# A long convolution beside a feed-forward on one core: copies of x and loads of w2 moved to later places in a planned order

## The chip, the cores and the metric

The kernel runs on one core of a Trainium2 chip. The metric is the device time of one execution in microseconds (us). Times are medians of several runs; the profile comes from one more execution, whose own time is given beside its span (from its first to its last instruction). The engines are TensorE (PE; PEld is its loading of weights), VectorE (DVE), ScalarE (ACT), GpSimd (POOL) and SyncE (SP). SP computes nothing here: it issues nearly all DMAs, in one queue, in order. POOL issues the DMAs that add into memory.

## The reference

The input x has 2048 rows of 1024 columns, in float32. Its rows are normalized (mean 0, variance 1), and two results are added to x:

```python
xn = _layernorm(x, axis=-1)
k_shift = 4-tap causal depthwise convolution of k        # per channel
kv = k_shift * v
y = causal depthwise convolution of kv with ssm_k        # 2048 taps, per channel, by FFT
a = xn * (y + kv * ssm_D)
b = silu(xn @ w1) @ w2                                   # 1024 -> 3584 -> 1024
return x + a + b
```

## The kernel before

**The feed-forward** is the work of TensorE. Every float32 operand is split into a high and a low float16 part, and three products stand for one. The first GEMM goes through w1 in 14 pairs of column tiles (`i`, 256 columns each) and the rows in two halves (`sp`, 1024 rows each). Most pairs run as a *unit*: seven products of sums of blocks (a Strassen scheme) in place of eight, 84 matmuls of 128x512 in all (`units`). The sums of x and w1, their split and the taking out of the products are work of VectorE and ScalarE. The order is two plain pairs for the first half, then 12 units for the first half, then 14 units for the second. `flag["unit", i]` is set where unit `i` of the second half begins. Hidden blocks go out to DRAM (`hs`, `hsf`) and come back as blocks `wo`.

The second GEMM begins when all units are done (`feed_forward`, from `flag["gemm1"]` on). It goes through the two column halves `h` of the result; in each, for 16 row tiles `t`, five blocks of 4 hidden tiles are summed in PSUM, and `result(h, t, ...)` scales the sum, and adds it into the result in DRAM (a POOL DMA with `accum_op`, helper `G`, L331 to L333). The last four pairs of hidden tiles follow as a second Strassen part (`units2`).

**The scale of w2.** Each pair of row tiles of w2 is scaled by a power of two that comes from the norms of w1 and w2. For the norms alone, `squares_w2` loads all of w2 once, in 28 pieces of 512 KB, into a buffer `wraw` or (for the first seven pairs) `yt`, and ScalarE squares and sums each piece. When all are done, `norms_w2` makes the scales (`tau`, `invc`), and then w2 is loaded once more (`load_w2`), scaled and split for the second GEMM.

**The convolution** goes in 8 groups of 128 channels. For one group k, v and the long filter are loaded; VectorE and ScalarE apply the taps and multiply with v (`gate`); the signal is split (`cm`) and turned by four transposing DMAs on SP's queue (helper `X`, L326 to L329, into `hl`); TensorE makes the first stage of a Fourier transform (`stage1`, L1490 to L1492); VectorE does the rest of it, the product and most of the inverse (`forward`, `product`, `inverse`, in the buffers `spec` and `tmp`); a norm sets the scale of the result (`result_scales`); the parts are split (`zh`, `zl`); TensorE does the last stage (`stage1_inv`, L1682 to L1684); VectorE multiplies with the scale and the normalized x (`gated`, into `yt`, `xg` being the rows of x), and POOL adds the 8 pieces of a group into the result. In the profile nearly all operations of VectorE have the lines of two helpers (L336, L339) and those of ScalarE one (L347), so they are told apart by buffer names.

**The result starts as a copy of x.** `copies` issues 16 DMAs from x to the result, each of 256 rows and one column half (512 KB): eight for the first column half, then eight for the second. `flag["copied", half]` lets the convolution's adds of that column half go ahead: groups 0 to 3 lie in the first half, 4 to 7 in the second.

**What sets the order.** All engines' instructions are written out by a planner (`Order`, L106 to L194). Each strand of work is a generator that yields an operation with a planned cost, or a condition to wait for. The planner always takes the strand whose next operation can begin first in its model, less a bias, and emits it. So a condition, or a planned cost, changes the place of everything after it, on all engines, though the engines themselves run only by their queues and semaphores. In the model a DMA occupies one common pipe for its `nbytes` at 330 GB/s. A strand's conditions are conditions of the planner alone: they set no semaphore.

Of the kernel before, what the change touches and what calls it, by code (L numbers as in the profile page):

```python
# [25 lines left out]
NT = S // P  # L26
# [79 lines left out]
class Order:  # L106
# [27 lines left out]
    def add(self, gen, bias, floor=0.0):  # L134
        s = Stream(gen, bias, floor)
        self.streams.append(s)
        self.advance(s)
# [151 lines left out]
def h3_ffn_kernel(ctx, tc, x, kp, vs, fs, shift, dskip, w1, w2, cfwd, cinv, out):  # L289
    nc = tc.nc  # L290
# [3 lines left out]
    flag = defaultdict(Token)  # L294
# [12 lines left out]
    def size(a):  # L307
        n = 1
        for s in a.shape[1:]:
            n *= s  # L310
        return n
# [10 lines left out]
    def L(o, i, m=0.3):  # L322
        n = size(o) * o.shape[0] * mybir.dt.size(o.dtype)
        return Op("SP", 0.4, 0.1, lambda: nc.sync.dma_start(o, i), [i], [o], m, n)

    def X(o, i, m=0.3):  # L326

        n = size(o) * o.shape[0] * mybir.dt.size(o.dtype)
        return Op("SP", 0.6, 0.1, lambda: nc.sync.dma_start(o, i, transpose=True), [i], [o], m, 1.5 * n)  # L329

    def G(o, i, m=0.3):  # L331
        n = size(i) * i.shape[0] * mybir.dt.size(i.dtype)
        return Op("POOL", 1.1, 3.0, lambda: nc.gpsimd.dma_start(o, i, accum_op=ADD), [i], [o], m, n)  # L333
# [8 lines left out]
    def a_act(o, i, func, scale=1.0, bias=None, total=None):  # L342
        def f():
            kw = {} if bias is None else {"bias": bias}
            if total is not None:
                kw["accum_out"] = total
            nc.scalar.activation(o, i, func, scale=scale, **kw)  # L347
        ins = [i] + [s for s in (scale, bias) if s is not None and not isinstance(s, float)]
        p = A(f, o, ins)
        p.table = func if func in (AF.Sqrt, AF.Silu) else None  # L350
        p.busy += 0.07 * (len(ins) - 1) - 0.06 * (i.space == bass.MemoryType.PSUM)
        if total is not None:
            p.busy += 0.19
            p.writes.append(total)
        return p
# [566 lines left out]
    def plain_unit(i, b, xf, ready, m=1, free=False):  # L922

        ph = []
        for j in range(2):
            yield ff.ready
            ph.append(ff.tile([P, 4, P]))
        for n, j in [(n, j) for n in range(m) for j in range(2)]:
            q = slice(n * 4 // m, (n + 1) * 4 // m)
            for a in range(2):  # L930
                for r in ready[a][n * len(ready[a]) // m:(n + 1) * len(ready[a]) // m]:
                    yield r
                yield flag["w", "plain", i, a, j]
                w, tok = wops["plain", i, a, j]
                yield from steps(ph[j][0][:, q, :], w, xf[a][:, q], a == 0, a == 1)
                if free and n == m - 1:
                    tok.set()
            if n == m - 1:
                if j == 0:
                    hf, both = yield from places_of(i, b)  # L940
                add(silu(i, hf[:, j], *ph[j], both), EB)
# [11 lines left out]
    def units():  # L953

        todo = [(i, 0) for i in range(2, NP)] + [(i, 1) for i in range(NP)]
        yield ff.ready
        one = ff.tile([P, 4, P])
        yield from product("P1", *todo[0], one[0], True)
        for n, (i, sp) in enumerate(todo):
            if sp == 1:  # L960
                flag["unit", i].set()
                flag["room", 1].set()
            if i in PAIRS:
                add(quad(i, sp), 0.1)
            made, seen = defaultdict(Token), defaultdict(Token)
            yield ff.ready
            c = ff.tile([P, 4, P])
            add(evacuate(i, 2 * sp, one, c, made, seen), EB)
            yield from product("P7", i, sp, c[0], True)
            yield seen["P1"]  # L970
            two = seen["bank"][0]
            yield from product("P6", i, sp, two)
            made["P6"].set()
            yield from product("P2", i, sp, one[0])
            made["P2"].set()
            yield seen["P6"]
            yield from product("P5", i, sp, two)
            made["P5"].set()
            if n + 1 < len(todo):
                yield ff.ready  # L980
                one = ff.tile([P, 4, P])
                yield from product("P1", *todo[n + 1], one[0], True)
            yield seen["P5"]
            yield from product("P3", i, sp, two)
            made["P3"].set()
            yield seen["P7"]
            yield from product("P4", i, sp, c[0])
            made["P4"].set()
# [13 lines left out]
    def feed_forward():  # L1002
        first = [xo[0]["A11"], xo[0]["A12"]]
        r = [flag["rows", t] for t in range(4)]
        yield from plain_unit(0, 0, first, (r, r), 2)
        yield from plain_unit(1, 0, first, ((), ()))
        yield flag["x", 0, "A22"]
        lower = [second["A21"], xo[0]["A22"]]
        r = [(flag["x", 0, "A21"],), (flag["x", 0, "A22"],)]
        yield from plain_unit(0, 1, lower, r, free=True)  # L1010
        yield from plain_unit(1, 1, lower, r, free=True)
        second["tok"].set()
        flag["room", 0].set()
        yield from units()
        flag["gemm1"].set()
        for h in range(2):
            for ts in TOGETHER[h]:
                pos = {}
                for c in range(NC):
                    for t in ts:  # L1020
                        if c == 0:
                            yield ff.ready
                            pos[t] = ff.tile([P, W])
                        yield flag["h", h, t, c]
                        hx, htok = flag["h", h, t, c].what
                        yield flag["w2", h, c]
                        wc, wtok = w2c[h, c]
                        yield from steps2(pos[t][0], hx, wc, c == 0, c == NC - 1)
                        htok.set()
                        if t == NT - 1:  # L1030
                            wtok.set()
                        if c == NC - 1:
                            add(result(h, t, *pos[t]), EB)
        flag["last part"].set()
        yield from units2()

# [4 lines left out]
    def steps2(po, hx, wc, first, last, more=False):  # L1041
        for n in range(4):
            def mm(n=n):
                kw = dict(skip_group_check=more)
                nc.tensor.matmul(po, hx[:, n, 0, :], wc[:, n, 0, :], start=first and n == 0, stop=False, **kw)  # L1045
                nc.tensor.matmul(po, hx[:, n, 0, :], wc[:, n, 1, :], start=False, stop=False, **kw)  # L1046
                nc.tensor.matmul(po, hx[:, n, 1, :], wc[:, n, 0, :], start=False, stop=last and n == 3, **kw)  # L1047
            yield T(mm, po, [hx[:, n], wc[:, n]], 3 * 0.2185)
# [112 lines left out]
    def result(h, t, po, tok):  # L1161
        yield vs_r.ready
        o, otok = vs_r.tile([P, W])
        yield a_act(o, po, AF.Copy, invc[:, 0:1])
        tok.set()
        yield G(orr[t // T2, t % T2, :, h * W:(h + 1) * W], o)
        otok.set()
# [14 lines left out]
            flag["h2", u, n].set()  # L1182

    def copies():
        for a in range(NT):
            yield flag["unit", a // 2]
            n = NT // 2
            q = slice(a % n * 2 * P, (a % n + 1) * 2 * P), slice(a // n * W, (a // n + 1) * W)
            o = out[q]
            yield Op("SP", 0.4, 0.1, lambda: nc.sync.dma_start(o, x[q]), [], [], 0.3, P * D * 4)  # L1190
            flag["copied", a // n].set()

    def squares_w2():

        yield lambda: "wraw" in ctxs
        for i in range(NP):
            for h in range(2):
                yield lambda: any(r.pairs() for r in ctxs["squares"][i])
                raw, tok = next(r for r in ctxs["squares"][i] if r.pairs()).pair([P, 2, W])
                yield L(raw, w2r[:, 2 * i:2 * i + 2, h * W:(h + 1) * W])  # L1200
                add(square_w2(raw, tok, ss2[:, i, h:h + 1]), 0.01)
# [3 lines left out]
    def square_w2(raw, tok, o):  # L1205
        yield a_act(raw, raw, AF.Square, total=o)
        tok.set()
        flag["w2 squares"].set()
# [556 lines left out]
    add(factors_w1(), 0.04)  # L1765
    add(spill_w1(), 0.0)
    add(feed_forward(), 0.0)
    add(load_x(), 0.06)
    add(load_h(), 0.05)
# [45 lines left out]
```

## Time and profile before

| | |
|---|---|
| median of 3 runs | 1280.41 us (1280.33 to 1281.85) |
| the profiled execution | 1279.35 us, span 1277.5 us |
| granted TensorE clock, mean | 0.989 |
| busy: PE, DVE, ACT, POOL | 1236.3, 1150.4, 729.8, 132.8 us |
| moved by DMA | 292.94 MB, mean 229 GB/s |

The first GEMM's matmuls run from 15 to 592 us, the first convolution group's first stage begins at 302.5 us, the last group's at about 1147 us. Busy times are of engines that work side by side; idle time of an engine costs only where another one waits for it. A row with `[1.52 <-ACT cm L347]` at its end says that the engine was idle for 1.52 us before it and which instruction ended that.

### The profile page before, as it was taken

How to read it: one execution, taken by the hardware profiler on the slowest of the kernel's cores; microseconds unless marked ns; L12 is line 12 of the kernel's file. 1: busy time of each engine (PE TensorE's matmuls, PEld its weight loads, DVE VectorE, ACT ScalarE, POOL GpSimd, SP SyncE). 2: the span in 40 equal slices, each digit the busy share in tenths (PEclk: the TensorE clock that was granted, in tenths of full speed). 3: DMA queues.
4: the chain of work that ended last, by engine and by line, in shares of the span. 5: the costliest groups of instructions: out<-in, count | busy, mean ns of one | idle time of the engine just before them, and what ended most of it. 6: DMA issues, size and time to landing. Idle time of an engine off the chain costs nothing.

```text
span 1277.5 us, 17092 instructions
## 1 busy us (share of the span) xinstructions
PE 1236.3 (97%) x6018; PEld 596.9 (47%) x6018; DVE 1150.4 (90%) x1533; ACT 729.8 (57%) x1169; POOL 132.8 (10%) x141
## 2 busy tenths in 40 slices
PE   7899999999899999999999999999999999999994
PEld 6544444444344454444444444444454454445442
DVE  8999997898599969999799979989979988998996
ACT  6867987777775577666654452364263246535232
POOL 0000000000000030000210120030030021112213
PEclk8999999999899999999999999999999999999998
DMA  9447899889999899888996696598677678977865
GB/s 329 157 158 230 269 323 313 287 261 344 340 367 303 283 268 291 242 237 278 321 293 159 152 224 148 105 279 265 138 162 205 148 156 257 232 168 143 156 107 75
DMA packets 253894, 292.94 MB, mean 229 GB/s; under 512 B 48752, under 2 KB 167536, under 8 KB 251632
## 3 DMA queue, kind: packets, MB, share of 16 engines
q1 hardware_dynamic: 227072, 266.93, 67.0%
q0 software_dynamic: 26736, 24.92, 15.1%
q8 instruction: 47, 0.77, 0.2%
q14 instruction: 39, 0.32, 0.1%
HBM read 193.22 MB, written 98.57 MB: 228 GB/s over the span
## 4 chain that ended last, share of the span: by engine, by line
PE 59%; DVE 21%; DMA 7%; issue 7%; ACT 2%; POOL 2%; SPq 0%; POOLq 0%; DVEq 0%; ACTq 0%
PE ff L918 12%; PE ff L919 12%; PE ff L917 12%; DVE spec L336 8%; PE ff L1045 6%; PE ff L1047 6%; PE ff L1046 6%; DVE tmp L336 3%; DMA out<-yt 2%; DVE spec L339 2%; POOL out L333 2%; DVE x L339 1%; PE ps L1490 1%; PE ps L1492 1%; PE ps L1491 1%
## 5 line engine op out<-in xcount | busy, mean ns | idle before, releaser
L1045 PE MATMUL ff<-x,wo 128*128 128x512 f16 x864 | 327.4, 379 | 2.9 <-ACT hf L347 1.7
L1046 PE MATMUL ff<-x,wo 128*128 128x512 f16 x864 | 327.4, 379 | 0.2 <-DVE x L339 0.2
L1047 PE MATMUL ff<-x,wo 128*128 128x512 f16 x864 | 327.4, 379 | 0.0
L917 PE MATMUL ff<-x,wo 128*128 128x512 f16 (+1 forms) x808 | 305.2, 378 | 2.0 <-ACT hf L347 1.8
L918 PE MATMUL ff<-x,wo 128*128 128x512 f16 (+1 forms) x808 | 305.1, 378 | 2.0 <-DVE x L339 2.0
L919 PE MATMUL ff<-x,wo 128*128 128x512 f16 (+1 forms) x808 | 305.1, 378 | 0.3 <-DVE wo L339 0.3
L336 DVE TENSOR_TENSOR spec<-spec 128x512 f32<-128x512 f32 (+2 forms) x256 | 261.4, 1053 | 2.2
L1046 PEld LDWEIGHTS <-wo 128*128 128x128 f16 x864 | 84.5, 98 | 103.0 <-issue 3.7
L1047 PEld LDWEIGHTS <-wo 128*128 128x128 f16 x864 | 84.5, 98 | 102.4 <-issue 0.5
L1045 PEld LDWEIGHTS <-wo 128*128 128x128 f16 x864 | 85.4, 99 | 99.7
L919 PEld LDWEIGHTS <-wo 128*128 128x128 f16 x808 | 79.7, 99 | 96.2 <-issue 3.5
L917 PEld LDWEIGHTS <-wo 128*128 128x128 f16 x808 | 81.3, 101 | 88.4 <-issue 0.8
L918 PEld LDWEIGHTS <-wo 128*128 128x128 f16 x808 | 79.8, 99 | 91.1 <-issue 3.3
L347 ACT ACTIVATE hf<-ff,invc 128x512 f32<-128x512 f32 x64 | 43.6, 682 | 117.5 <-PE ff L1047 80.4
L333 POOL DMA_DIRECT2D out<-yt x62 | 69.5, 1312 | 344.3 <-DVE yt L339 200.8
L333 POOL DMA_DIRECT2D out<-hf x63 | 56.1, 890 | 459.3 <-ACT hf L347 393.7
L336 DVE TENSOR_TENSOR tmp<-spec 128x2048 f32<-128x2048 f32 (+1 forms) x48 | 92.4, 1934 | 1.0
L347 ACT ACTIVATE spec<-spec 128x1024 bf16<-128x1024 f32 x32 | 33.8, 1055 | 81.1 <-DVE spec L336 81.0
L339 DVE SCALAR_TENSOR_TENSOR ht<-hf,wsc,ht 128x1024 f16<-128x1024 f32 (+1 forms) x56 | 67.4, 1204 | 11.0 <-ACT ht L347 10.8
L339 DVE SCALAR_TENSOR_TENSOR acc<-kin,taps,acc 128x1024 f32<-128x1024 f32 x48 | 61.5, 1281 | 11.9 <-ACT acc L347 11.4
L347 ACT ACTIVATE ht<-hf,wsc 128x1024 f16<-128x1024 f32 (+1 forms) x56 | 60.8, 1085 | 6.0 <-DMA hsfA<-ht 2.6
L347 ACT ACTIVATE spec<-ps 128x512 f32<-128x512 f32 x93 | 52.7, 588 | 18.7 <-PE ps L1492 17.9
(177 smaller groups left out, 1744.0 us busy)
## 6 DMA issues: line engine op xcount, KB each, us to landing
wo<-hs SPq DMA_DIRECT2D x160, 256.0 KB, 3.5
hs<-ht SPq DMA_DIRECT2D x80, 256.0 KB, 5.2
out<-hf POOLq DMA_DIRECT2D x63, 256.0 KB, 4.3
wraw<-in_w SPq DMA_DIRECT2D x30, 512.0 KB, 5.9
raw<-in_w SPq DMA_DIRECT2D x28, 512.0 KB, 5.8
kin<-in_kp SPq DMA_DIRECT2D x16, 704.0 KB, 6.0
xt<-in_x SPq DMA_DIRECT2D x16, 512.0 KB, 7.4
kf<-in_fs SPq DMA_DIRECT2D x8, 1024.0 KB, 7.0
```

The lines of the kernel that those rows point to most:

```text
L333: return Op("POOL", 1.1, 3.0, lambda: nc.gpsimd.dma_start(o, i, accum_op=ADD), [i], [o], m, n)
L336: return V(lambda: nc.vector.tensor_tensor(o, a, b, op=op), o, [a, b], **k)
L339: return V(lambda: nc.vector.scalar_tensor_tensor(o, a, s, b, op0=op0, op1=op1), o, [a, b] + ([] if isinstance(s, float) else [s]), **k)
L347: nc.scalar.activation(o, i, func, scale=scale, **kw)
L917: nc.tensor.matmul(o, w[:, 0, k], xf[:, :, k, 0], start=first and k == 0, stop=False, **kw)
L918: nc.tensor.matmul(o, w[:, 0, k], xf[:, :, k, 1], start=False, stop=False, **kw)
L919: nc.tensor.matmul(o, w[:, 1, k], xf[:, :, k, 0], start=False, stop=last and k == KH - 1, **kw)
L1045: nc.tensor.matmul(po, hx[:, n, 0, :], wc[:, n, 0, :], start=first and n == 0, stop=False, **kw)
L1046: nc.tensor.matmul(po, hx[:, n, 0, :], wc[:, n, 1, :], start=False, stop=False, **kw)
L1047: nc.tensor.matmul(po, hx[:, n, 1, :], wc[:, n, 0, :], start=False, stop=last and n == 3, **kw)
L1490: nc.tensor.matmul(o, cf[:, 0], hi[i], start=i == 0, stop=False, **kw)
L1491: nc.tensor.matmul(o, cf[:, 0], lo[i], start=False, stop=False, **kw)
```

## The change

Three edits, of which the last two are new conditions for the planner and the first a planned cost:

- The transposing DMA is planned with its own bytes instead of 1.5 times as many.
- The copies into the second column half no longer follow the units; copy number `a - 8` of that half waits until the plan has added `result(0, t)` for row tile `t = a - 8` of the first column half.
- The loads of w2 for its norms wait for `flag["unit", 2]`, the begin of the third unit of the second half.

```diff
     def X(o, i, m=0.3):
 
         n = size(o) * o.shape[0] * mybir.dt.size(o.dtype)
-        return Op("SP", 0.6, 0.1, lambda: nc.sync.dma_start(o, i, transpose=True), [i], [o], m, 1.5 * n)
+        return Op("SP", 0.6, 0.1, lambda: nc.sync.dma_start(o, i, transpose=True), [i], [o], m, n)
...
                         if c == NC - 1:
                             add(result(h, t, *pos[t]), EB)
+                            if h == 0:
+                                flag["result", t].set()
...
     def copies():
+        n = NT // 2
         for a in range(NT):
-            yield flag["unit", a // 2]
-            n = NT // 2
+            yield flag["unit", a // 2] if a < n else flag["result", a - n]
             q = slice(a % n * 2 * P, (a % n + 1) * 2 * P), slice(a // n * W, (a // n + 1) * W)
             o = out[q]
             yield Op("SP", 0.4, 0.1, lambda: nc.sync.dma_start(o, x[q]), [], [], 0.3, P * D * 4)
...
     def squares_w2():
 
         yield lambda: "wraw" in ctxs
+        yield flag["unit", 2]
         for i in range(NP):
```

## The prediction

> **What bounds the kernel now.** I read the page first, then the end of the chain of work that ended last, then the busy times by stretch of the span, and last the waits inside the stretches that stand out.
>
> ```profile
> span 1277.5 us, 17092 instructions
> PE 1236.3 (97%) x6018; PEld 596.9 (47%) x6018; DVE 1150.4 (90%) x1533; ACT 729.8 (57%) x1169; POOL 132.8 (10%) x141
> PE 59%; DVE 21%; DMA 7%; issue 7%; ACT 2%; POOL 2%; SPq 0%; POOLq 0%; DVEq 0%; ACTq 0%
> ```
>
> By share TensorE (PE) is the bound, with 41 us idle in all. But the chain spends 21% on VectorE (DVE), so the end has to be read by itself. These are pieces of the chain there (start, length, what):
>
> ```profile
> 1254.26 2.27 DVE spec L336 x2
> 1256.53 1.21 DVE zl L339
> 1257.78 0.27 PE ps L1683
> 1260.39 0.69 DVE yt L339
> 1261.45 0.53 POOL out L333
> ...
> 1269.30 2.19 POOL out L333 x2
> 1271.49 0.93 POOLq L1811
> ```
>
> The last thing to happen is the eighth and last convolution group: VectorE finishes its inverse transform, splits it (zl), TensorE multiplies, VectorE gates (yt), and GpSimd (POOL) adds the pieces into the result one after the other. From the split at 1256.53 to the end of the span is 21 us of tail in a fixed order. So the time is "when does VectorE reach the last split", plus that tail. VectorE doesn't pause before it, as the last two rows of the next view show; its idle time lies earlier. The columns are stretch, its length, busy time of PE, PEld, DVE, ACT and POOL with instruction counts, granted clock, DMA share, GB/s:
>
> ```profile
> core 0: us, PE busy (x) PEld busy (x) DVE busy (x) ACT busy (x) POOL busy (x), PEclk, DMA share, GB/s
> 288.00:320.00 32.00, 32.00 (x151) 14.47 (x148) 26.89 (x36) 24.28 (x34) 0.00 (x0) 1.00 1.10 343
> 320.00:352.00 32.00, 28.44 (x120) 12.19 (x119) 16.00 (x20) 25.49 (x44) 0.76 (x1) 0.89 1.09 340
> 352.00:384.00 32.00, 32.00 (x151) 14.63 (x150) 31.86 (x31) 21.84 (x37) 0.00 (x0) 1.00 1.04 368
> 448.00:480.00 32.00, 31.80 (x172) 16.63 (x171) 20.25 (x24) 25.34 (x43) 9.75 (x9) 1.00 1.11 268
> 576.00:608.00 32.00, 29.82 (x144) 13.89 (x142) 31.89 (x37) 22.06 (x26) 0.00 (x0) 1.00 0.90 277
> 1184.00:1216.00 32.00, 32.00 (x150) 14.52 (x149) 30.96 (x27) 7.09 (x12) 6.85 (x9) 1.00 0.81 158
> 1216.00:1248.00 32.00, 32.00 (x152) 14.63 (x150) 31.35 (x40) 9.83 (x17) 5.91 (x7) 1.00 0.55 96
> ```
>
> The reader is to see two holes in VectorE's work: 320 to 352 us (idle 32 - 16.00 = 16.0 us) and 448 to 480 us (11.75 us). Both lie where the DMA engines are full (shares 1.09 and 1.11) and where the moved loads and copies stand. The first also costs TensorE: 120 matmuls instead of 151, and its clock drops to 0.89.
>
> ```profile
> PE ps L1490 <- DMA hl<-cm: 3.6, 1, 3.6
> ...
> 320.00:328.00 8.00, 5.99 (x28) 2.54 (x26) 4.88 (x8) 4.87 (x10) 0.00 (x0) 1.00 1.15 351
> 328.00:336.00 8.00, 6.45 (x18) 2.44 (x19) 2.64 (x3) 5.85 (x10) 0.76 (x1) 0.57 1.02 347
> 336.00:344.00 8.00, 8.00 (x38) 3.62 (x37) 4.36 (x5) 7.13 (x11) 0.00 (x0) 1.00 1.12 292
> ```
>
> TensorE waited once, 3.6 us, for a transposing DMA of the first convolution group; then its clock was 0.57 over 8 us. Together 10 + 20 matmuls are missing against the 38 of the third row: at 8.00 / 38 = 0.21 us each 6.3 us, of which 3.6 are the wait and 2.7 the clock. [...]
>
> **The change, part by part.** Nothing is added or dropped: the same 16 copies, 28 loads of w2 and 28 squares. Three things move, and the written-out order of every engine moves with them; I take that order from the two programs as built. It holds no times.
>
> *A. The loads of w2 for the norms begin later.* The first stands behind 1437 products (128x512 matmuls of the feed-forward) instead of 1311. So the first hole loses these ScalarE (ACT) squares, of which the answers for the two target buffers show four rows each (two squares, each with its reading of the sum):
>
> ```profile
> 320.00:352.00 32.00, 0.00 (x0) 2.28 (x4) 0.89 1.09 340
> 320.00:352.00 32.00, 0.00 (x0) 2.27 (x4) 0.00 (x0) 0.89 1.09 340
> ...
> 315.50 0.39 SPq L324 DMA_DIRECT2D wraw<-in_w  x1
> 315.93 0.48 SPq L324 DMA_DIRECT2D yt<-in_w  x1
> 316.46 0.92 SPq L1190 DMA_DIRECT2D out<-in_x  x1
> ...
> 323.45 3.31 SPq L329 DMA_TRANSPOSE hl<-cm  x1
> ...
> 317.00 0.75 DVE L339 SCALAR_TENSOR_TENSOR cm<-acc,csc,cm 128x512 f16<-128x512 f32 x1 [1.52 <-ACT cm L347]
> ```
>
> Squares: 2.28 + 2.27 = 4.55 us of ScalarE, in a stretch where VectorE's waits end on ScalarE. The transpose: its data were ready at 317.75, the queue of SP issued it at 323.45. Two w2 loads go from in front of it: 0.87 us of issue, and 1 MB, 3.1 us at 340 GB/s. Together 4.0 us, more than the 3.6 us that TensorE waited. The gain for VectorE lies between 0 (another input of the same chain is late) and 10.9 us (idle time falls to the 5.1 us of the stretch before). I take the squares whole and half of the wait, as both partly fill the same hole: 4.55 + 1.8 = 6.35 us. What is late next is the rest of that chain, the ScalarE splits and the copies that stay.
>
> *B. Eight copies of x leave the second hole.* In the old order the last two stand here:
>
> ```profile
> 448.84 6.21 DMA out<-in_x
> 455.05 8.98 DMA out<-yt
> ...
> 464.15 1.41 DVE L339 SCALAR_TENSOR_TENSOR yt<-ps,csc,xg 128x512 f32<-128x512 f32 x2 [1.02 <-DMA out<-yt]
> ...
> 462.44 0.69 DVE L336 TENSOR_TENSOR tmp<-tmp,ps 128x512 f32<-128x512 f32 x1 [2.32 <-ACT spec L347]
> 469.66 0.69 DVE L336 TENSOR_TENSOR spec<-spec,ps 128x512 f32<-128x512 f32 x1 [3.51 <-ACT spec L347]
> ...
> out<-yt POOLq DMA_DIRECT2D x62, 128.0 KB, 5.9
> ```
>
> An add into the result that follows the copies took 8.98 us instead of the median 5.9, and VectorE waited 1.02 us for it. The other waits of this hole are for ScalarE and TensorE, and no copy is in them. Between 0 and 3.1 us; I take the wait shown, 1.0.
>
> *C. Where they go.* The copies now stand one by one behind 2527 to 2917 products, each behind a result of the first column half: in time about 633 to 730 us. Behind a copy on SP's queue are the loads of hidden blocks (wo) and of the next group; the copies carry no wait for another engine in the built order, so only their issue and bandwidth count:
>
> ```profile
> 590.00:635.00 45.00, 43.55 (x225) 21.84 (x224) 38.68 (x42) 32.28 (x42) 7.43 (x7) 1.00 1.04 310
> 635.00:730.00 95.00, 93.15 (x446) 43.40 (x444) 90.40 (x103) 43.29 (x80) 10.87 (x12) 1.00 0.76 203
> ```
>
> There is room for 4.2 MB: 203 GB/s against 310 to 340, so 95 us have 10 MB to spare. What remains is the stretched add of part B, now for the third group: cost 0 to 3.1 us, taken 1.0. [...]
>
> *D. The squares stand closer.* From first to last square there were 888 products, now 785, so 12% denser, and the second hole gets about one more square of 1.2 us beside its waits for ScalarE: cost 1.2, between 0 and 3.5 (the longest of those waits doubled once).
>
> *E. The planner's price of a transposing DMA falls by a third.* No instruction changes; it shifts order. The last group's norm stands behind 4955 products instead of 4992, and the third to seventh groups' norms 39 to 46 products earlier, while VectorE's own order there differs by one instruction at most. So TensorE comes to each group's matmuls 37 x 0.21 = 8 us earlier than before. That is no gain in itself; it lets VectorE's gain through up to about 8 us, and turns what VectorE doesn't gain into waits of TensorE, which had nothing to wait for before.
>
> Sum: 6.35 + 1.0 - 1.0 - 1.2 = 5.15 us. The profiled execution took 1279.35 us (span 1277.5 and 1.85 around it), so 1274.2; the median of the runs, 1280.41, is 1.06 above it: **1275.3 us**.
>
> **The rivals.**
>
> *More than that.* The first hole closes to the level of its neighbour: 10.9 us gained, 1269.5. For it: the stretch after it runs at 31.86 of 32 with the DMA engines as full. Against: the copies, spills and splits of the first group stay.
>
> *Nothing.* VectorE's waits only move: the hole's real cause is the start of the first group beside the last weights, and the squares fall on the start of the second. 1280.4, within 2 us. For it: DMA shares of 1.04 to 1.11 on both sides of 352 us.
>
> *Slower, by TensorE's order.* VectorE gains nothing and TensorE, 8 us early by order, waits at the convolution's matmuls. Waits in themselves replace idle time later; what is lost is the clock. Price: 2.7 us for each wait like the one at 329. The point from which it decides lies between 2.2 us idle (576 to 608, PE 29.82, clock 1.00) and 3.6 (clock 0.57). With two such waits, one at the second group's end and one where the first blocks of w2 are split, 5.4 us: 1285.8. [...]
>
> *Slower, by a late norm.* If the squares, started later, end late, every block of w2 is scaled late and the second GEMM starts late.
>
> ```profile
> L347 ACT ACTIVATE wraw<-wraw x21: 1034/1044/1060, 323.9 to 543.8; 128x1024 f32<-128x1024 f32 x21
> L347 ACT ACTIVATE x<-wraw,tau x16: 706/1134/1150, 570.5 to 1091.9; 128x1024 f16<-128x1024 f32 x9, 128x512 f16<-128x512 f32 x7
> wraw<-in_w SPq DMA_DIRECT2D x30, 512.0 KB, 5.9
> ```
>
> A buffer takes 5.9 + 1.0 + 0.2 = 7.1 us a square; 14 squares on two buffers and 14 on one take 14 x 3.6 + 14 x 7.1 = 150 us, and 785 products are 165. That leaves 15 us, and between the last square and the first scaled block lie 27 us, in which one load of 5.9 us and the norm stand. It decides when the squares end over 10 us late, and then costs the rest, some 5 us: 1285.
>
> That the change doesn't do what it says can be left out: the built order shows loads and copies in their new places.
>
> **How the numbers follow.** Forecast, a gain of 3 to 8 us: 0.41. More: 0.17. Nothing (within 0.2%, 2.6 us, about what a measurement of this kernel can tell from no change): 0.15. Slower by TensorE's order 0.17, by a late norm 0.10. So faster 0.58, same 0.15, slower 0.27. The range must reach into both ends: down to a gain of 12 us, 1268, and up to the slower cases' prices, 1286. The forecast's own range is 1272 to 1277.5.
>
> **What would show it.** Right: the stretch 320 to 352 with VectorE near 22 busy and 1.00 clock, no wait for the transposing DMA, the last zl split near 1251. A: squares gone from ScalarE before 355. B and C: the first add's landing near 6 us, and adds of the third group near 700 us longer than 5.9. D: VectorE's waits for ScalarE between 450 and 480 as long as before. E: waits of TensorE for VectorE at the convolution's matmuls in every group, each under 3 us. Wrong: a second dip of the clock after 350 us, a last square later than 555, or VectorE's idle time before 480 as large as it is now.

## The result, and the profile after

The changed kernel takes 1271.13 us (median of 9 runs, 1266.17 to 1274.45) against 1278.15 us for the kernel before, run beside it (9 runs, 1275.97 to 1281.85). The ratio is 0.9938, with an interval of 0.9919 to 0.9956: a gain of 7.0 us. The forecast was 5.15 us of gain and 1275.3 us. The measured time lies 4.2 us below the forecast one and 0.9 us below the forecast's own range of 1272 to 1277.5; of these 4.2 us, 2.3 are the kernel before, which took 1278.15 us here against the 1280.41 that the forecast started from. The profiled execution of after took 1272.2 us, span 1270.4, clock 0.992.

The page of after, by the lines that were read of before:

```profile
span 1270.4 us, 17081 instructions
PE 1234.8 (97%) x6018; PEld 595.6 (47%) x6018; DVE 1150.0 (91%) x1533; ACT 734.2 (58%) x1169; POOL 132.9 (10%) x141
PE 24%; DVE 19%; issue 8%; DMA 6%; ACT 2%; POOL 2%; SPq 0%; POOLq 0%; DVEq 0%; ACTq 0%
```

Busy times have hardly moved (VectorE 1150.4 to 1150.0 us): the same work, with less idle time between. The end of its chain of waits still runs through VectorE's last gating (yt), POOL's adds and the last add's issue:

```profile
1260.93 0.77 DVE yt L339
...
1262.11 2.19 POOL out L333 x2
```

The stretches of the span that the prediction named (columns as there):

```profile
320.00:352.00 32.00, 30.47 (x142) 13.67 (x140) 20.85 (x26) 22.80 (x40) 0.76 (x1) 1.00 1.00 300
448.00:480.00 32.00, 29.80 (x156) 15.17 (x155) 23.52 (x26) 24.87 (x46) 9.73 (x9) 1.00 1.07 270
624.00:632.00 8.00, 5.19 (x24) 2.24 (x23) 8.00 (x8) 4.48 (x8) 0.00 (x0) 0.97 1.11 334
632.00:640.00 8.00, 8.00 (x31) 3.28 (x30) 7.97 (x9) 5.61 (x12) 0.89 (x1) 0.81 1.06 365
```

In the first hole VectorE is busy 20.85 us instead of 16.00, TensorE runs 142 matmuls instead of 120, and the clock stays at 1.00. The second hole is fuller too (23.52 instead of 20.25). A dip of the clock appears at another place, 632 to 640 us.

**One sum that carries the rest.** The prediction read the time as "when does VectorE reach the last split, plus a tail". That can be tested on all 14 profiled executions of this study: take the start of the last split of a convolution group in the trace (the last row of VectorE that writes zl), and VectorE's idle time up to there. Span less that idle time is 1162.2 us in before, 1162.6 in after, and between 1160.4 and 1163.0 in all 14, while the spans run from 1265.3 to 1279.5 us. So the span is VectorE's idle time before the last split plus about 1162 us, and the question is only where VectorE idles.

To see that, the views below cut each trace where VectorE has done 270, 350, 500, 650, 940 and 1140 us of work. Each stretch then holds the same amount of VectorE's work in every kernel, and its length less its busy time is idle time. The first stretch, up to 294 us, is left out: it has 24 us of idle time in both. The columns are stretch, length, VectorE's busy time with its instructions, granted clock, DMA share, GB/s. Before:

```profile
294.01:395.10 101.09, 80.00 (x94) 0.97 1.08 346
395.10:558.75 163.65, 150.00 (x181) 1.00 0.93 270
558.75:720.02 161.27, 150.01 (x176) 1.00 0.87 248
720.02:1036.31 316.29, 290.00 (x336) 1.00 0.73 181
1036.31:1255.05 218.74, 200.00 (x236) 1.00 0.79 173
```

After:

```profile
294.35:389.97 95.62, 80.00 (x94) 1.00 1.03 336
389.97:551.50 161.53, 150.00 (x175) 1.00 0.88 256
551.50:707.51 156.01, 150.00 (x183) 0.99 0.95 278
707.51:1030.27 322.76, 290.00 (x335) 1.00 0.73 182
1030.27:1247.41 217.14, 200.00 (x236) 1.00 0.78 176
```

Stretch by stretch, after less before: -5.5 (the first hole), -2.1 (the second hole), -5.3 (where the blocks of w2 are first scaled), +6.5 (the ends of groups three to five), -1.6 (the last stretch: the end of group six, group seven, and group eight up to its splits). With +0.3 ahead of them that is 7.6 us less, for a span that is 7.1 us shorter. So the first hole's gain is there. But another 5.3 us was won and 6.5 us lost in places that the prediction didn't price, and only experiments can tell which edit did which.

### The profile page after: what moved, and what is told of

It is laid out like the page before. It is cut to its first block, busy times and chain, and to the rows that moved or that the text cites. A ratio compares the mean times of both kernels' runs of the same rounds, so it can differ in the third digit from the quotient of the medians.

```text
span 1270.4 us, 17081 instructions
## 1 busy us (share of the span) xinstructions
PE 1234.8 (97%) x6018; PEld 595.6 (47%) x6018; DVE 1150.0 (91%) x1533; ACT 734.2 (58%) x1169; POOL 132.9 (10%) x141
## 4 chain that ended last, share of the span: by engine, by line
PE 24%; DVE 19%; issue 8%; DMA 6%; ACT 2%; POOL 2%; SPq 0%; POOLq 0%; DVEq 0%; ACTq 0%
DVE spec L336 7%; PE ff L1048 7%; PE ff L1047 7%; PE ff L1049 7%; DVE tmp L336 3%; POOL out L333 2%; DVE ht L339 1%; DMA hf<-in_w 1%; DVE x L339 1%; DVE acc L339 1%; DMA kin<-in_kp 1%; DVE spec L339 1%; DMA out<-yt 1%; PE ps L1493 1%; PE ps L1495 1%
## 5 line engine op out<-in xcount | busy, mean ns | idle before, releaser
L333 POOL DMA_DIRECT2D out<-yt x64 | 72.4, 1300 | 344.0 <-DVE yt L339 204.3
```

## The experiments

Each kernel is the kernel before with the edits shown. Every ratio is against runs of the kernel before beside it, whose medians were 1276.77 us (for sq_only, cp_only, x_only, sq_cp), 1276.69 (sq_x, cp_x, all_three, sq_price2) and 1275.62 (the last four). Those of sq_x, cp_x, all_three and sq_price2 are from one chip, the others from a second one; each ratio is between runs on the same chip. A length by stretch comes from one execution, which mostly lies within 2.5 us of its kernel's median (4.9 in cp_only; that of before lies 1.2 us above its median in the comparison with after and 2.6 to 3.7 above the three medians here); the ratios decide, the stretches tell where. In kernels with added lines the line numbers are a few higher.

### The three edits, each alone: sq_only, cp_only, x_only

sq_only moves only the loads of w2 for the norms:

```diff
         yield lambda: "wraw" in ctxs
+        yield flag["unit", 2]
```

> Only the loads of w2 for the norms wait for the third unit; copies and the planned price of the transposing DMA as before. In its planned order the last group's norm stands behind 12 products fewer than before (37 fewer in the changed kernel). Theory H (the gain is made in the stretch 320 to 352 us, where squares leave ScalarE and loads leave the queue ahead of the transposing DMA): VectorE's busy time in that stretch is 20 to 22 us as in the changed kernel, the 3.6 us wait and the clock dip are gone, and the time falls by 4 to 6 us. Theory O (what counts is how early TensorE meets the convolution in the planned order; 12 of 37 products): falls by 2 to 3 us. Theory C (the copies made the gain): within 1.5 us of before.

Measured: 1276.75 us, ratio 1.0000 (0.9988 to 1.0012). No gain at all. Yet the first hole is filled, and the squares are gone from it. Its stretch 320 to 352, then its stretches by VectorE's work:

```profile
320.00:352.00 32.00, 29.95 (x132) 13.18 (x131) 21.40 (x26) 23.43 (x42) 0.76 (x1) 0.95 1.01 311
```

```profile
293.88:390.09 96.21, 80.00 (x94) 0.98 1.01 330
390.09:554.07 163.98, 150.00 (x172) 1.00 0.95 284
554.07:710.54 156.47, 150.00 (x186) 1.00 0.89 256
710.54:1031.69 321.15, 290.00 (x336) 1.00 0.72 181
1031.69:1255.16 223.47, 200.00 (x236) 0.99 0.76 169
```

Against before: -4.9 in the first hole, +0.3, -4.8, then +4.9 and +4.7. VectorE enters the last stretch at 1031.69 instead of 1036.31 us and leaves it at 1255.16 instead of 1255.05. The whole gain has been given back by then. In the last stretch VectorE waits for these (engine, line, what it waited for, us, times, longest), in sq_only:

```profile
DVE yt L339 <- DMA out<-yt: 8.2, 4, 4.7
DVE spec L336 <- ACT spec L347: 4.2, 2, 3.1
DVE tmp L336 <- ACT spec L347: 3.0, 5, 0.9
```

and in before:

```profile
DVE yt L339 <- DMA out<-yt: 7.3, 4, 3.8
DVE tmp L336 <- ACT spec L347: 2.6, 5, 0.6
...
DVE spec L336 <- ACT spec L347: 1.8, 2, 1.3
```

No single wait took it back: the landings of adds (out), the spectra (spec, tmp) and others are each waited for a little longer.

cp_only moves only the copies into the second column half (the edits of `feed_forward` and `copies`).

> Only the eight copies into the second column half move behind the first half's results. In its planned order the last group's norm stands behind as many products as before. Theory H: the stretch 320 to 352 us stays as before (VectorE about 16 us busy, clock under 0.95), 448 to 480 us gains 1 to 3 us, adds of the third group cost about as much later: time within 2 us of before. Theory O: no change, within 1.5 us. Theory C: falls by 5 us or more.

Measured: 1275.95 us, 0.9998 (0.9984 to 1.0012). Nothing.

x_only changes only the planned price of a transposing DMA:

```diff
-        return Op("SP", 0.6, 0.1, lambda: nc.sync.dma_start(o, i, transpose=True), [i], [o], m, 1.5 * n)
+        return Op("SP", 0.6, 0.1, lambda: nc.sync.dma_start(o, i, transpose=True), [i], [o], m, n)
```

> Only the planned price of the transposing DMA falls by a third: no load or copy is told to move. In its planned order the last group's norm stands behind as many products as before, some groups' by 35 to 44 fewer. Theory H and theory C: within 1.5 us of before. Theory O: within 1.5 us of before too; a gain of 4 us or more would mean that the price alone carries it, which none of the three says.

Measured: 1281.36 us, 1.0038 (1.0024 to 1.0052): slower. So no edit alone brings anything, and the three ratios together would be a small loss. The gain of 0.6% is an interaction.

### Two edits together: sq_cp, sq_x, cp_x, and all three again

sq_cp has loads and copies, with the old price.

> The loads of w2 and the copies move as in the change, the planned price of the transposing DMA stays as before. In its planned order the last group's norm stands behind 37 products fewer, just as in the changed kernel. Theory H: gain of 5 to 8 us, as the changed kernel within 1.5 us. Theory O: as the changed kernel, about 7 us. Theory C: as the copies alone.

Measured: 1275.37 us, 0.9986 (0.9971 to 1.0). At most a small part.

sq_x has loads and price, with the copies as before.

> Loads of w2 later and the transposing DMA priced lower, copies as before. Last group's norm 37 products earlier, as in the changed kernel; the groups before it too (39 to 48). Theory O (the filled hole pays only if TensorE's order is moved by as much): 5 to 7 us faster. Theory C2 (copies beside the first adds cost the rest): 2 to 4 us faster, as the copies still stand in 448 to 480 us, and the changed kernel beats it by 3 us or more.

Measured: 1268.16 us, 0.9927 (0.9909 to 0.9944).

cp_x has copies and price, with the loads as before.

> Copies later and the transposing DMA priced lower, loads of w2 as before. Last group's norm behind as many products as before, and the hole at 320 to 352 us not filled. Theory O and theory H: within 2 us of before, or slower by up to 5 us as the price alone was. A gain of 4 us or more would mean that the loads of w2 have no part in it.

Measured: 1279.14 us, 1.0014 (1.0 to 1.0027).

all_three is the changed kernel once more, beside them.

> The changed kernel once more, on the same chip as the three next ones. Its planned order has the last group's norm 37 products earlier than before. Expected by every theory: 6 to 8 us faster than before, as in the first comparison. If it falls below 4 us, part of that first difference was the chip's.

Measured: 1267.98 us, 0.9936 (0.9913 to 0.996). So the copies play no part that can be measured, and the gain is that of the loads together with the price. The stretches of sq_x show where the pair differs from the loads alone:

```profile
293.46:388.50 95.04, 80.00 (x94) 1.00 1.05 338
388.50:551.13 162.63, 149.99 (x172) 1.00 0.94 283
551.13:705.82 154.69, 150.00 (x186) 1.00 0.90 259
705.82:1025.96 320.14, 290.00 (x335) 1.00 0.71 181
1025.96:1242.31 216.35, 200.01 (x237) 1.00 0.76 175
```

Against sq_only: -1.2, -1.3, -1.8, -1.0, -7.1. The price takes a little off everywhere, and 7.1 us in the last stretch.

### Which groups' price: sq_price2, sq_hole, sq_later

The order in which the program was written out offered a ready explanation: in after the last group's norm stands 37 products earlier, in sq_only 12. sq_price2 moves the loads and lowers the price for the first two groups only (8 transposing DMAs); its last norm stands where it stood before, 0 products earlier.

```diff
+    turned = []
...
-        return Op("SP", 0.6, 0.1, lambda: nc.sync.dma_start(o, i, transpose=True), [i], [o], m, 1.5 * n)
+        turned.append(1)
+        return Op("SP", 0.6, 0.1, lambda: nc.sync.dma_start(o, i, transpose=True), [i], [o], m, n if len(turned) <= 8 else 1.5 * n)
...
         yield lambda: "wraw" in ctxs
+        yield flag["unit", 2]
```

> Loads of w2 later; the lower price of the transposing DMA holds for the first two groups only, copies as before. The stretch 320 to 352 us is filled as with the loads alone (VectorE 20 to 22 us busy), but the planned order ends with the last group's norm behind as many products as before (0 fewer, groups 5 to 7 9 to 12 fewer). Theory O: no gain, within 1.5 us of before, and some waits of VectorE for TensorE's matmuls after 900 us. Against theory O: 4 us or more faster.

Measured: 1268.97 us, 0.9935 (0.9912 to 0.9957). The whole gain without the shift; and sq_cp, with all 37 products, had hardly any. The theory that TensorE's earlier place in the order lets VectorE's gain through has fallen.

sq_hole lowers the price for the first group only (`<= 4`): it differs from sq_only in SP's queue in the first hole.

> The loads of w2 for the norms later, the lower price of the transposing DMAs for the first convolution group alone, copies as before. Against the kernel with the later loads alone, the first group's second transposing DMA stands in front of a load of 1 MB of x on SP's queue instead of behind it, and the last group's norm stands 12 products earlier than before, as there. Theory Q (the gain is made in the first hole, by this place in SP's queue): TensorE loses under 2.5 us between products 1300 and 1420 and the time is 6 to 9 us under before, ratio 0.993 to 0.995. Rival L (the gain is made later, by the order of the second group and what follows it): TensorE loses little in the hole as well, but the time stays within 2.5 us of before, ratio 0.998 to 1.002. Rival O (order of the last group): ratio near 1, as 12 products are no more than with the later loads alone.

Measured: 1275.43 us, 0.9995 (0.9975 to 1.0014). SP's queue there, in sq_only and then in sq_hole (start, issue time):

```profile
303.28 1.24 SPq L324 DMA_DIRECT2D x<-xspS  x1
304.61 3.79 SPq L329 DMA_TRANSPOSE hl<-cm  x1
```

```profile
301.40 6.84 SPq L332 DMA_TRANSPOSE hl<-cm  x1
308.34 0.53 SPq L324 DMA_DIRECT2D x<-xspS  x1
```

The second transposing DMA goes in front of a load of 1 MB, 3.2 us earlier. The stretch of the first hole gets 1.2 us shorter by it than in sq_only; here it is with the last stretch:

```profile
293.89:388.91 95.02, 80.00 (x94) 1.00 1.05 338
...
1026.71:1249.12 222.41, 200.00 (x236) 1.00 0.76 171
```

The time does not follow, since the last stretch is nearly as long (222.41) as with the loads alone (223.47). (This execution took 1273.01 us, 2.4 below its kernel's median.) So the lower price in the first hole alone is not enough.

sq_later is the complement, the lower price for all groups but the first (`> 4`).

> The complement: the loads of w2 later, the lower price for all groups but the first, copies as before. In the first hole SP's queue is that of the kernel with the later loads alone; from the second group on the order is near that of the kernel with loads and price. Theory Q: TensorE loses near 4 us between products 1300 and 1420, ratio 0.998 to 1.001. Rival L: ratio 0.993 to 0.995 in spite of the hole. If both this kernel and the one before it gain about half (0.996 to 0.997), both places count and the sum of the two is the whole.

Measured: 1270.99 us, 0.995 (0.9931 to 0.997), with the first hole's stretch of sq_only to the hundredth. It and the last stretch:

```profile
293.57:389.78 96.21, 80.00 (x94) 0.98 1.02 330
...
1028.31:1244.34 216.03, 200.00 (x237) 1.00 0.76 176
```

The last stretch is 7.4 us shorter than in sq_only. The theory of the hole's queue falls and the rival, the order from the second group on, holds. sq_price2 and sq_later, which gain, have the second group's price in common, and sq_hole, which doesn't have it, gains nothing. (sq_hole, sq_later and sq_only ran on the same chip.)

### Smaller dose, and more copies out of the hole: sq_x_u1, sq_x_copies_late

sq_x_u1 is sq_x with `flag["unit", 1]`: the loads begin one unit earlier.

> As the kernel with the later loads and the lower price, copies as before, but the loads of w2 begin at the second unit of the second half instead of the third: a smaller dose. The norms of the groups four to eight return to within 9 products of the order of before. Theory Q: what counts is whether squares and their loads are out of 320 to 352 us; some come back, VectorE is busy there 18 to 20 us, and the ratio is 0.995 to 0.998. Rival L (the order of the later groups): with the later groups' order that of before, nothing is left, 0.999 to 1.001.

Measured: 1270.75 us, 0.9952 (0.9933 to 0.9971). Most of the gain, with the norms of groups four to eight within 9 products of their places in before. That is within what was expected of a smaller dose in the hole, and the rival's 0.999 to 1.001 did not come: whatever counts in the order from the second group on, it is not the place of the later groups' norms. But the reason given with it is wrong too: VectorE's busy time in the hole did not fall to 18 to 20 us, it rose over the 21.90 of sq_x:

```profile
320.00:352.00 32.00, 31.49 (x147) 14.16 (x145) 23.26 (x27) 25.57 (x45) 0.76 (x1) 1.00 1.06 325
```

Its squares begin at 340.0 us, so a few of them inside the hole do no harm.

sq_x_copies_late is sq_x with all 16 copies two units later, so that those into the first column half leave the first hole as well:

```diff
-            yield flag["unit", a // 2]
+            yield flag["unit", 2 + a // 2]
```

> As the kernel with the later loads and the lower price, and all 16 copies of x two units later than before, so that those into the first column half leave the first hole too. If copies in the hole still hold the first group's transposing DMAs back, VectorE is busy over 22 us between 320 and 352 and the time is 1 to 3 us under that of the kernel without this edit (ratio 0.990 to 0.992). If copies play no part, as the runs with the moved second half say, the ratio stays at 0.992 to 0.994. A loss (over 0.995) would come from adds into the result that wait for the later copies.

Measured: 1275.45 us, 0.9991 (0.9973 to 1.0009). It loses the whole gain of sq_x. Both things that were expected happened, in different stretches:

```profile
294.51:386.12 91.61, 80.00 (x95) 1.00 0.99 321
386.12:556.13 170.01, 150.00 (x172) 0.99 0.93 282
```

The first hole is 3.4 us shorter than in sq_x (95.04), the next stretch 7.4 us longer (162.63). There VectorE waits once for 5.4 us until an add into the result has landed, a wait that sq_x does not have there:

```profile
DVE yt L339 <- DMA out<-yt: 5.4, 1, 5.4
```

No version clearly beats the changed kernel: sq_x (0.9927) and all_three (0.9936) have overlapping intervals.

## Why the prediction came out as it did

**What sets the end** was read rightly: VectorE's way to the last splits and a tail in fixed order. The last group has four splits. They begin between 1256.5 and 1261.0 us in before and between 1247.6 and 1253.1 in after. The prediction's 1256.53 is the first of them; it came 8.9 us earlier, and the tail from there to the end of the span grew from 21.0 to 22.8 us. By that measure about 1251 was forecast and 1247.6 came, and the tail is not of fixed length. The idle time before the last split accounts for the span of every kernel here within 1.3 us of the middle.

**A, the loads of w2.** The mechanism was right, and so was its size in its stretch: 6.35 us expected, 5.5 measured in after and 4.9 for the loads alone; the clock stayed at 1.00 in after, TensorE's wait for the transposing DMA is gone, and the squares start at 359.6 us:

```profile
L347 ACT ACTIVATE wraw<-wraw x21: 1037/1044/1077, 359.6 to 547.3; 128x1024 f32<-128x1024 f32 x21
```

What failed is the step from the hole to the end, "what is late next is the rest of that chain". The loads alone gave 1.0000: what was late next lay 400 us and more further on, in groups three to eight. The half of the wait for the transposing DMA was put at 1.8 us; the DMA's earlier place in the queue was worth 1.2 us of the hole (sq_hole against sq_only) and nothing of the time.

**B and C, the copies.** Priced at +1.0 and -1.0, and together they are nothing: all_three and sq_x can't be told apart. B took the wait of 1.02 us for an add as what the copies cost. With the copies gone that wait did not go: between 435 and 485 us VectorE waits in after for

```profile
DVE yt L339 <- DMA out<-yt: 3.1, 1, 3.1
```

and for such a landing also in all_three (1.9 us) and sq_cp (4.4), while sq_x, with the copies in their old place, has no such wait. The first group's adds did mostly land faster: between 440 and 485 us their median is 7.1 to 8.2 us in the eight kernels with the copies in their old place and 4.4 to 7.5 in the five without. But VectorE's stretch there is no shorter for it in cp_only (idle 15.4 us, before 13.7) and 1.1 us shorter in after than in sq_x. sq_x_copies_late shows the other end: copies pushed into that stretch made it 7.4 us longer.

In C the third group's adds land a little later, as said. Their median between 700 and 760 us, of before and then after:

```profile
out<-yt POOLq DMA_DIRECT2D x8, 128.0 KB, 5.9
```

```profile
out<-yt POOLq DMA_DIRECT2D x8, 128.0 KB, 6.6
```

By itself that doesn't say that the copies beside them slowed the adds: the same median is 6.0 to 6.6 us in the five kernels with copies in that part and 5.1 to 6.8 in the nine without (5.1 in sq_only, 6.8 in sq_x_copies_late). So for the third group's adds no run here shows that a copy beside them slows them.

**D, the denser squares,** was priced at 1.2 us. The second hole's stretch got shorter instead, by 2.1 us in after, and with the loads alone it stayed (+0.3). The cost was not found.

**E, the lower price,** is the step that failed. The prediction said "That is no gain in itself", which x_only bears out with a loss of 0.38%; and that it "lets VectorE's gain through" by putting TensorE 37 products earlier. The runs contradict the second: full gain at 0 products (sq_price2), nearly none at 37 (sq_cp). Nor did TensorE's waits grow in exchange: at the convolution's matmuls it waited for VectorE or ScalarE seven times in before (6.6 us in all) and five times in after (5.1 us). What stands in its place: with the loads moved, the lower price of the second group's transposing DMAs (the one thing that sq_price2 and sq_later share and sq_hole lacks) changes the order from there on, and VectorE then idles less in the last stretch (23.5 us in sq_only and 22.4 in sq_hole; 16.0 to 16.6 in sq_later, sq_x, sq_price2 and all_three, 17.1 in after; only in sq_x_u1 it is 19.0, beside a first hole 3.0 us shorter than in sq_only). That it acts through what the planner writes out, the order and with it the choice of buffers, is certain, as the price is a number of the planner alone. Which of the moved instructions does it stays open: the waits that shrink are many and small, and the lower price for the second group alone was not tried. One marker is worth following: of the kernels with moved loads, the six that gain start their last square at 545.8 to 550.4 us, and three that don't at 553.8 (sq_hole), 556.6 (sq_only) and 564.2 (sq_x_copies_late). But sq_cp starts it at 549.1 and hardly gains, and nothing was followed from there to a wait of the last stretch, so it is a marker and no shown cause. A second one fits the last stretch, narrowly, in all ten kernels with moved loads: sq_only, sq_hole and sq_cp scale 17 blocks of w2 out of the buffer wraw and 19 out of hf, and VectorE idles 19.6 to 23.5 us there; the other seven scale 16 and 20, and it idles 16.0 to 19.0 us. This too was not followed to a wait.

**What was in no step.** 5.3 us were won where the blocks of w2 are first scaled. In before VectorE waited there for ScalarE's part of the blocks, between 605 and 680 us,

```profile
DVE x L339 <- ACT x L347: 7.1, 5, 2.4
```

and in after between the same times mostly for a spectrum:

```profile
DVE spec L336 <- ACT spec L347: 2.7, 2, 1.8
```

Part of it goes in x_only too, which moves no load (158.10 us against 161.27), and the next stretch gives as much back (319.25 against 316.29). So these 5.3 us and the 6.5 us lost behind them say little about the loads: much of both comes with any new order.

**The rivals.** *Nothing* describes the loads alone, and the forecast's sign came from a partner that the prediction had costed at nothing. So that the gain came out at 7.0 us for 5.15 is luck: the 6.35 us of A, which make the sum, do not reach the end by themselves (ratio 1.0000), and E, without which there is no gain, is in no term of it. *Slower by a late norm*: in after the last square starts 3.5 us later than before (547.3 against 543.8), far from the 10 us from which it was to cost. In sq_only it starts 12.8 us later, yet the first scaled block comes no later (568.2 us against 570.5 in before), so the mechanism was not seen there either. *Slower by TensorE's order* expected dips of the clock at waits between 2.2 and 3.6 us; after has one dip after 350 us, at 632 us, which the prediction had named as a sign of being wrong, and gains all the same. The two bounds don't hold: the 2.2 us between 576 and 608 are several waits, the longest of 1.8 us, and the dip in after follows two waits of 1.6 and 1.3 us. The last section shows after which idle times the clock dropped in three of the executions.

## What to carry to other kernels

Find the engine whose last piece of work starts the tail, cut the traces of both kernels at equal amounts of that engine's work, and compare the stretches: a filled hole counts only if no later stretch has grown. Where a planner writes out the order, a changed planned price is an edit of every later instruction; test it with each other edit before calling it free. And one edit at a time is not enough to divide a gain: here each of three alone gave nothing or a loss, and one pair gave all of it.

## What the runs showed of the hardware that was not expected

**TensorE's clock dropped after the shorter of two waits and not after the longer.** In sq_only TensorE waited twice by the same view, for 2.0 us near 328 us and for 3.5 us near 608 us:

```profile
PE ff L917 <- DVE hf L336: 2.0, 1, 2.0
```

```profile
PE ps L1491 <- ACT spec L347: 3.5, 1, 3.5
```

The drop after the shorter one is one step of 3.41 us, from 330.48 us. In before and in after the drops between the start and 1250 us begin and end whole multiples of 3.413 us from one another, within 0.003 us (the last of them lasts from 328.06 to 334.88 us in before and from 631.59 to 635.01 in after). So each trace is cut here in steps of that length, counted from its own drop. These are sq_only's steps around the two waits (the number after the length is TensorE's busy time, the third number from the end the clock):

```profile
327.07:330.48 3.41, 1.36 (x7) 0.55 (x6) 3.34 (x5) 3.41 (x8) 0.76 (x1) 1.00 0.86 287
330.48:333.89 3.41, 3.41 (x10) 1.21 (x8) 0.03 (x1) 1.95 (x3) 0.00 (x0) 0.50 1.09 250
606.96:610.37 3.41, 1.49 (x7) 0.59 (x6) 2.03 (x2) 3.21 (x4) 0.00 (x0) 1.00 1.03 405
610.37:613.79 3.42, 1.83 (x9) 0.88 (x9) 2.85 (x3) 3.24 (x6) 0.81 (x1) 1.00 1.08 385
```

The shorter wait lies whole in one step, which is idle for 3.41 - 1.36 = 2.05 us, and the next step runs at 0.50. The longer is divided, 1.92 and 1.59 us, and nothing follows. The steps around the drops of before and then after:

```profile
324.64:328.05 3.41, 1.35 (x7) 0.39 (x4) 2.65 (x5) 1.76 (x5) 0.00 (x0) 1.00 1.29 315
328.05:331.47 3.42, 1.92 (x5) 0.74 (x6) 2.50 (x3) 3.42 (x7) 0.00 (x0) 0.50 1.03 307
331.47:334.88 3.41, 3.41 (x9) 1.21 (x8) 0.14 (x1) 2.38 (x4) 0.76 (x1) 0.50 1.03 381
```

```profile
628.18:631.59 3.41, 0.87 (x4) 0.19 (x2) 3.41 (x4) 1.15 (x1) 0.00 (x0) 1.00 1.08 378
631.59:635.01 3.42, 3.15 (x8) 1.13 (x8) 3.42 (x5) 1.97 (x3) 0.00 (x0) 0.50 1.06 390
```

In before the wait of 3.6 us is divided into 2.06 and 1.50 us, and both steps are followed by one at 0.50. In after two waits, of 1.6 and 1.3 us, make one step idle for 2.54 us, and the next is at 0.50. The other steps of these two executions from 60 to 1250 us are idle for at most 1.82 us, and none of them is followed by a drop. The ends of matmuls are modelled, so these idle times are as good as that model. In none of the three executions was a step that a drop followed idle throughout.

**In one pair of executions a transposing DMA that was issued 3.2 us earlier left the queue only 0.16 us earlier.** By the rows of the hole above, it holds SP's queue from 304.61 for 3.79 us in sq_only and from 301.40 for 6.84 us in sq_hole: until 308.40 and 308.24 us. The 1 MB load that it was put in front of was issued 5 us later for it (308.34 against 303.28). What it waited for in the queue, the trace does not say.
